# A chunked delta rule with a GELU feed-forward: chunks of 64 tokens with two batches on the partitions, and 32x32 diagonal blocks inverted row by row on VectorE

## The chip, the cores and the metric

The kernel runs on one core of a Trainium2 chip. A core has five engines that matter here: TensorE (PE in the profile; its weight loads are listed apart as PEld), VectorE (DVE), ScalarE (ACT), GpSimd (POOL) and SyncE (SP, which here only issues DMAs). Each engine runs its own instructions in order and waits for the others by semaphores. The metric is the device time of one execution in microseconds (us). All arithmetic is in float32.

## The reference

```python
def _attn_ref(q, k, v, beta):                      # q, k, v: (4, 8, 768, 48), beta: (4, 8, 768)
    B, H, S, D = q.shape
    k_n = k / (np.linalg.norm(k, axis=-1, keepdims=True) + 1e-06)
    state = np.zeros((B, H, D, D), dtype=np.float32)
    y = np.zeros_like(q)
    for t in range(S):
        kt, vt, bt = (k_n[:, :, t], v[:, :, t], beta[:, :, t, None])
        y[:, :, t] = np.einsum('bhd,bhde->bhe', q[:, :, t], state)
        v_old = np.einsum('bhde,bhd->bhe', state, kt)
        state = state + bt[:, :, :, None] * np.einsum('bhd,bhe->bhde', kt, vt - v_old)
    return y

def _moe_ref(x, w_in, w_out):                      # x: (3072, 384), w_in: (384, 2048), w_out: (2048, 384)
    h = x @ w_in
    g = 0.5 * h * (1.0 + erf(h * np.float32(1.0 / np.sqrt(2.0))))
    return g @ w_out

# y is laid out as x: (B, H, S, D) -> (B*S, H*D)
```

The first part is a recurrence over 768 tokens for each of 32 batch-and-head pairs, with a 48x48 state; the second is a feed-forward over 3072 rows. Both kernels take the recurrence in chunks of C tokens. With N[j, i] = beta_j k_j.k_i and P[j, i] = k_j.q_i for j < i (0 elsewhere), and the state St at the chunk's start, a chunk is

    (I + N^T) U = V - K St,   W = beta U,   Y = Q St + P^T W,   St' = St + K^T W.

So each chunk and head needs the inverse of a unit triangular C x C matrix, or rather that inverse transposed, Z, as the left operand of a matmul.

## The kernel before

A chunk is 128 tokens, on the 128 partitions. There are 6 chunks, 4 batches and 8 heads. A unit is one batch's chunk with its 8 heads; a group is two units (two batches), 12 groups in all.

For each unit, `prep` takes the norms of K (GpSimd and VectorE) and writes the normed K; `transposed` turns K and Q with eight TensorE transposes (L200) and ScalarE copies them out; `grams` forms K K^T and K Q^T (psG, L211), which VectorE (L216) scales by beta and masks to N, and ScalarE and GpSimd (L220, L222) copy and mask to P.

The inverse is then built on TensorE by doubling, from blocks of 1 to blocks of 64: at each of six sizes, `join` forms the part of M X that the size joins (psI, masked by VectorE at L244), `update_x` and `update_z` form X M X and its transpose (psI), and VectorE subtracts them (L268, L270, L273). The two 64x64 diagonal blocks of a head lie one above the other on the partitions and use two diagonal quarters of the TensorE array. `last_join` and `last_z` (L280, L289) join 64 to 128. All psI matmuls but the last are issued in the helper at L231.

The state of a chunk runs through `against_state` (psK, L314, and W, L317), `solve` (psU, L322, and U, L325), `read` (psY, L345 and L349), `next_state` (psS, L334, and the state's sum, L338) and `turn` (psX, L357, which turns the unit's result into columns of xT). The feed-forward of a group is `fc1` (psH, L372, 16 times 3 matmuls of 256 columns, then GELU on ScalarE) and `fc2` (psO, L381, 16 matmuls of 384 columns for each unit).

The order is made in two steps. `interleave` merges lists of steps by their place in each list: while group i runs through its state, group i + 1 is inverted and group i - 1 is in the feed-forward. From that program the framework makes each engine's own order. At the start the weights arrive as float64 words and are decoded to float32 by five VectorE and two GpSimd instructions each (`decode`, L167 to L175), 28 pieces, between the first two groups' inverses:

```python
    interleave(inverse_steps(0), [(decode, n) for n in range(n_in)])
    load(2)
    interleave(state_steps(0), inverse_steps(1), [(decode, n) for n in range(n_in, NW)])
    for i in range(1, NG):
        load(i + 2)
        interleave(state_steps(i), inverse_steps(i + 1), ffn_steps(i - 1))
    interleave(ffn_steps(NG - 1))
```

## Time and profile before

| what | us |
|---|---|
| median of three runs | 1407.06 |
| lowest and highest of the three | 1398.52, 1407.37 |
| span of the profiled execution (first to last instruction) | 1391.1 |
| first matmul of the first group's state (psU) starts at | 108.6 |
| VectorE busy in 108 to 200 us | 69.4 of 92 |
| VectorE busy in 400 to 500 us | 33.3 of 100 |
| DMA, mean share of the 16 engines in 400 to 500 us | 0.07 |

The profile is of one execution; its span leaves out what lies before the first and after the last instruction. A group's row names line, engine, operation, output and inputs, contraction rows by output rows, the moving operand's shape and the count, then busy time, mean duration in ns, and idle time before it with what ended it. A timeline row gives start, duration, and how many instructions it merges. A row of the windows view gives the stretch, then busy time and count of PE, PEld, DVE, ACT and POOL, then the granted TensorE clock (1.00 is full speed), the share of the DMA engines and GB/s.

### The profile page before, as it was taken

How to read it: one execution, taken by the hardware profiler on the slowest of the kernel's cores; microseconds unless marked ns; L12 is line 12 of the kernel's file. 1: busy time of each engine (PE TensorE's matmuls, PEld its weight loads, DVE VectorE, ACT ScalarE, POOL GpSimd, SP SyncE). 2: the span in 40 equal slices, each digit the busy share in tenths (PEclk: the TensorE clock that was granted, in tenths of full speed). 3: DMA queues.
4: the chain of work that ended last, by engine and by line, in shares of the span. 5: the costliest groups of instructions: out<-in, count | busy, mean ns of one | idle time of the engine just before them, and what ended most of it. 6: DMA issues, size and time to landing. Idle time of an engine off the chain costs nothing.

```text
span 1391.1 us, 37806 instructions
## 1 busy us (share of the span) xinstructions
PE 1338.4 (96%) x17806; PEld 1097.2 (79%) x17806; DVE 513.9 (37%) x964; ACT 178.8 (13%) x386; POOL 218.9 (16%) x217
## 2 busy tenths in 40 slices
PE   2979889999999999999999999999999999999999
PEld 1879778778878878878878877887887887887876
DVE  5785874423323332342342343342332233333100
ACT  1101011021011102102102102102101110210211
POOL 8554461101101001011010010110100100100000
PEclk9985989999998998999998999999899899999999
DMA  8322220010010001001001001001000000000000
GB/s 148 91 86 69 83 57 13 14 30 8 10 33 7 8 13 30 2 19 29 3 19 24 8 14 29 8 13 30 7 2 13 1 3 7 7 2 8 6 12 12
DMA packets 82571, 33.97 MB, mean 24 GB/s; under 512 B 75728, under 2 KB 78800, under 8 KB 82416
## 3 DMA queue, kind: packets, MB, share of 16 engines
q1 hardware_dynamic: 78912, 26.75, 8.7%
q10 hardware_dynamic: 3504, 4.82, 1.0%
q8 instruction: 139, 2.28, 0.7%
q14 instruction: 16, 0.13, 0.0%
HBM read 26.84 MB, written 4.72 MB: 23 GB/s over the span
## 4 chain that ended last, share of the span: by engine, by line
PE 90%; DVE 5%; POOL 3%; ACT 1%; issue 1%; ACTq 0%; POOLq 0%
PE psI L231 28%; PE psH L372 20%; PE psO L381 19%; PE psG L211 8%; PE psU L322 4%; PE psY L349 3%; PE psI L289 2%; PE psI L280 2%; POOL w_e L171 2%; PE psY L345 1%; PE psT L200 1%; PE psK L314 1%; PE psX L357 1%; DVE w_e L173 1%; PE psS L334 1%; DVE X L268 1%
## 5 line engine op out<-in xcount | busy, mean ns | idle before, releaser
L372 PE MATMUL psH<-xT,w_in_sb 128*128 128x256 f32 x1152 | 303.3, 402 | 0.0
L381 PE MATMUL psO<-w_out_sb,g 128*128 128x384 f32 x768 | 268.7, 496 | 0.0
L372 PEld LDWEIGHTS psH<-xT,w_in_sb 128*128 128x128 f32 x1152 | 209.6, 194 | 32.9
L381 PEld LDWEIGHTS psO<-w_out_sb,g 128*128 128x128 f32 x768 | 139.2, 190 | 84.3
L244 DVE TENSOR_TENSOR T<-psI,join 128x512 f32<-128x512 f32 x144 | 99.1, 688 | 182.0 <-PE psI L231 181.5
L231 PEld LDWEIGHTS psI<-T,Z 64*64 64x64 f32 x3456 | 121.5, 135 | 34.2 <-issue 21.5
L231 PEld LDWEIGHTS psI<-Z,T 64*64 64x64 f32 x3840 | 122.6, 136 | 26.7 <-issue 17.4
L231 PE MATMUL psI<-Z,T 64*64 64x64 f32 x3840 | 135.6, 220 | 7.7 <-DVE T L244 3.6
L231 PE MATMUL psI<-T,Z 64*64 64x64 f32 x3456 | 136.8, 221 | 5.6 <-DVE X L268 3.3
L231 PEld LDWEIGHTS psI<-X,N 64*64 64x64 f32 x3840 | 120.4, 136 | 22.0 <-issue 15.7
L231 PE MATMUL psI<-X,N 64*64 64x64 f32 x3840 | 131.1, 221 | 3.8 <-DVE X L268 3.5
L375 ACT ACTIVATE g<-psH 128x256 f32<-128x256 f32 x192 | 73.7, 384 | 473.3 <-PE psH L372 473.3
L268 DVE TENSOR_TENSOR X<-X,psI 128x512 f32<-128x512 f32 (+1 forms) x120 | 82.2, 685 | 134.4 <-PE psI L231 133.7
L211 PE MATMUL psG<-KQt 48*128 48x128 f32 x768 | 119.2, 329 | 1.2
L211 PEld LDWEIGHTS psG<-KQt 48*128 48x128 f32 x768 | 103.5, 226 | 13.9 <-ACT KQt L201 4.0
L191 POOL TENSOR_TENSOR Kp<-K,rn 128x384 f32<-128x384 f32 x24 | 19.9, 831 | 467.5 <-PE psS L334 466.4
L222 POOL TENSOR_SCALAR_AFFINE_SELECT P<-P 128x1024 f32<-128x1024 f32 x24 | 26.3, 1094 | 403.5 <-ACT P L220 403.5
L270 DVE TENSOR_TENSOR Z<-Z,psI 128x512 f32<-128x512 f32 x96 | 65.9, 687 | 58.0 <-PE psI L231 58.0
L216 DVE SCALAR_TENSOR_TENSOR N<-psG,beta_sb,mask_u 128x128 f32<-128x128 f32 x192 | 53.0, 343 | 72.3 <-PE psG L211 71.4
L171 POOL TENSOR_SCALAR w_e<-w_e 128x384 uint32<-128x384 uint32 (+1 forms) x28 | 53.8, 1921 | 71.2 <-DVE w_e L167 70.3
L273 DVE TENSOR_TENSOR ZF<-Z,psI 64x512 f32<-64x512 f32 x48 | 32.9, 685 | 61.9 <-PE psI L231 61.6
L231 PE MATMUL psI<-ident_c,N 64*64 64x64 f32 x768 | 45.9, 260 | 7.9 <-DVE N L216 7.9
(75 smaller groups left out, 1014.5 us busy)
## 6 DMA issues: line engine op xcount, KB each, us to landing
w_raw<-in_moe_w_in_dram SPq DMA_DIRECT2D x12, 512.0 KB, 3.7
w_raw<-in_moe_w_out_dram SPq DMA_DIRECT2D x16, 384.0 KB, 3.1
K<-in_k_dram SPq DMA_DIRECT2D x24, 192.0 KB, 3.1
Qp<-in_q_dram SPq DMA_DIRECT2D x24, 192.0 KB, 3.5
V<-in_v_dram SPq DMA_DIRECT2D x24, 192.0 KB, 3.0
out_dram<-o_sb ACTq DMA_DIRECT2D x24, 192.0 KB, 1.9
bt<-in_beta_dram ACTq DMA_DIRECT2D x1, 96.0 KB, 3.0
```

Of the source, the lines that this page charges most:

```text
L171: nc.gpsimd.tensor_scalar(e, e, 896.0, 1151.0, op0=ALU.max, op1=ALU.min)
L211: nc.tensor.matmul(psG[:, j, :], lhsT=u.KQt[pr, 0, j, :], rhs=u.KQt[pr, a, j, :], start=True, stop=True)
L216: nc.vector.scalar_tensor_tensor(u.N[:, hh, j, :], psG[:, j, :], beta_sb[:, u.c, u.b, h:h + 1], mask_u, ALU.mult, ALU.mult)
L231: nc.tensor.matmul(psI[HALF[g], n, :], lhsT=lhsT(g, n), rhs=rhs(g, n), start=True, stop=True)
L244: nc.vector.tensor_tensor(u.T, psI, joins[s].unsqueeze(1).to_broadcast([128, H, HB]), op=ALU.mult)
L268: nc.vector.tensor_tensor(u.X[pr], u.X[pr], dX[pr], op=ALU.subtract)
L270: nc.vector.tensor_tensor(u.Z, u.Z, psI, op=ALU.subtract)
L322: nc.tensor.matmul(psU[:, h, :], lhsT=ZF[u.slot][:, (h % 2) * NP + h // 2, :], rhs=u.W[:, h, :], start=True, stop=True)
L349: nc.tensor.matmul(psY[:, h, :], lhsT=u.P[:, h % 2, h // 2, :], rhs=u.U[:, h, :], start=(u.c == 0 and h == 0), stop=True, skip_group_check ...
L372: nc.tensor.matmul(psH, lhsT=w_in_sb[:, m, f * 128:(f + 1) * 128], rhs=xTs[i][:, m, :], start=(m == 0), stop=(m == NM - 1))
L375: nc.scalar.activation(gs[f], psH, ACT.Gelu)
L381: nc.tensor.matmul(u.psO, lhsT=gs[f][:, u.n * C:(u.n + 1) * C], rhs=w_out_sb[:, f, :], start=(f == 0), stop=(f == NF - 1))
```

## The change

A chunk has 64 tokens, so there are 12 chunks, and a unit holds the same chunk of two batches, one on partitions 0 to 63 and one on 64 to 127. A chunk has two units (four batches), and the work goes chunk by chunk. Two neighbouring chunks form a group of the inverse: 4 units x 8 heads = 32 places, each with two batches and two 32x32 diagonal blocks of N.

`flip` transposes on VectorE, for each of the four quarters of the partitions, 32 blocks of 32x32 in one instruction (L254), so that a partition then holds one block of one place as a 32x32 matrix along its free dimension. `eliminate` inverts all 128 blocks at once, row by row: for j from 1 to 30 one multiply (L261) and one add (L263) over (31 - j) j elements. `back` turns the result back, into Z (L275) and, for the upper blocks, into XM (L277). `join` then makes the off-diagonal 32x32 block of each 64x64 inverse with two levels of 32x32 matmuls on TensorE (psJ, L297 and L300), copied out by ScalarE (L306, L309). The six doubling steps, the joins to 128 and their masks go.

N and P are both masked by VectorE out of one pair of banks (L241, L243); the mask times minus beta is made by GpSimd (L214). A gram matmul is 64 rows of output and 128 columns (K and Q side by side). All state matmuls (psK L334, psU L345, psY L355 and L360, psS L372) work on 64 partitions, two or four tiles in turn. K is loaded straight into its padded tile and normed in place, with six such tiles (three chunks); `load` of chunk c + 2 is called at the start of chunk c, and its K tiles are those of chunk c - 1. Each load and each store is split in two, one for each batch. The staging of the first weights lies in the tile of the second weights; a decode writes in place.

`interleave` now takes a weight for each step, and merges by the sums of weights. The elimination of the next group stands in odd chunks, beside the state of the chunk, the grams of chunk c + 2 and the feed-forward of chunk c - 1. The feed-forward (psH L400, psO L409) does what it did, on 12 groups.

```diff
-    C = 128
-    HB = 64
-    SIZES = (1, 2, 4, 8, 16, 32)
+    C = 64
+    HB = 32
...
+    def fetch_in(dst, src, u):
+        rows = slice(u.c * C, (u.c + 1) * C)
+        for p in range(2):
+            nc.sync.dma_start(out=dst[HALF[p]],
+                              in_=src[2 * u.a + p, :, rows, :].rearrange("h t d -> t h d"))
+
+    def load(c):
+        if c >= NC:
+            return
+        for a in range(NA):
+            u = tiles[c, a] = Unit()
+            u.c, u.a, u.n = c, a, c * NA + a
+            u.t = (c % 2) * NA + a
+            u.Kp, u.Qp, u.bm = Kp[u.n % NKS], Qp[u.n % NQS], bm[u.n % 2]
+            fetch_in(u.Kp[:, :, 0:D], k, u)
+            fetch_in(u.Qp[:, :, 0:D], q, u)
...
+    def prep(c):
+        us = [tiles[c, a] for a in range(NA)]
+        rn = wk.tile([128, NA * H], F32, tag="rn", name="rn")
+        for u in us:
+            kd = u.Kp[:, :, 0:D]
+            ksq = wk.tile([128, H, D], F32, tag="ksq", name="ksq")
+            nc.gpsimd.tensor_tensor(ksq, kd, kd, op=ALU.mult)
+            nc.vector.tensor_reduce(rn[:, u.a * H:(u.a + 1) * H], ksq, axis=AX.X, op=ALU.add)
+        nc.gpsimd.tensor_tensor(rn, rn, half, op=ALU.pow)
+        nc.vector.tensor_scalar_add(rn, rn, 1e-6)
+        nc.vector.reciprocal(rn, rn)
+        for u in us:
+            kd = u.Kp[:, :, 0:D]
+            nc.gpsimd.tensor_tensor(
+                kd, kd, rn[:, u.a * H:(u.a + 1) * H].unsqueeze(2).to_broadcast([128, H, D]),
+                op=ALU.mult)
+        for u in us:
+            nc.gpsimd.tensor_tensor(
+                u.bm, mask_h, beta_m[:, u.c, u.a].unsqueeze(2).to_broadcast([128, H, C]),
+                op=ALU.mult)
+    def transposed(u):
+        u.KQt = wk.tile([128, NP, 2, 2, C], F32, tag="KQt", name="KQt", bufs=6)
+        psT = dn("psT").rearrange("q b (j n) -> q b j n", j=NP)
+        for x, src in ((0, u.Kp), (1, u.Qp)):
+            flat = src.rearrange("q h d -> q (h d)")
+            for j in range(NP):
+                nc.tensor.transpose(psT[:, x, j, :], flat[:, j * 128:(j + 1) * 128], ident)
+        for x in range(2):
+            nc.scalar.copy(u.KQt[:, :, :, x, :],
+                           psT[:, x].rearrange("q j (p n) -> q j p n", p=2))
...
+        psG = dn("psG").rearrange("q r (j n) -> q r j n", j=NP)
+        for j in range(NP):
+            for r, p in QUADS:
+                rows = slice(r * C, r * C + D)
+                nc.tensor.matmul(psG[HALF[p], r, j, :], lhsT=u.KQt[rows, j, p, 0, :],
+                                 rhs=u.KQt[rows, j, p].rearrange("q x n -> q (x n)"),
+                                 start=True, stop=True)
+        nc.vector.tensor_tensor(heads(Ns[g][:, u.t]), psG[:, :, :, 0:C], heads(u.bm),
+                                op=ALU.mult)
+        nc.vector.tensor_tensor(heads(u.P), psG[:, :, :, C:], heads(mask_h), op=ALU.mult)
+
+    def eliminate_steps(g):
+        steps = []
+
+        def flip(qd):
+            if qd == 0:
+                Nus[g] = wk.tile([128, HB, HB], F32, tag="Nu", name="Nu", bufs=1)
+            rows = slice(qd * HB, (qd + 1) * HB)
+            cols = slice((qd % 2) * HB, (qd % 2 + 1) * HB)
+            src = Ns[g][rows].rearrange("q t h n -> q (t h) n")[:, :, cols]
+            nc.vector.transpose(Nus[g][rows], src.rearrange("q u n -> q n u"))
+
+        def eliminate(j):
+            nu = Nus[g]
+            n = HB - 1 - j
+            tmp = wk.tile([128, HB * HB // 4], F32, tag="tmp", name="tmp")
+            tmp = tmp[:, 0:n * j].rearrange("q (i c) -> q i c", i=n)
+            nc.vector.tensor_tensor(tmp, nu[:, j + 1:, j:j + 1].to_broadcast([128, n, j]),
+                                    nu[:, j:j + 1, 0:j].to_broadcast([128, n, j]), op=ALU.mult)
+            nc.vector.tensor_tensor(nu[:, j + 1:, 0:j], nu[:, j + 1:, 0:j], tmp, op=ALU.add)
+
+        def diagonal():
+            flat = Nus[g].rearrange("q i c -> q (i c)")
+            nc.vector.memset(flat[:, 0:HB * HB:HB + 1], 1.0)
+
+        def back(qd):
+            nu = Nus[g]
+            if qd == 0:
+                XMs[g] = wk.tile([128, NU, HB], F32, tag="XM", name="XM", bufs=1)
+            rows = slice(qd * HB, (qd + 1) * HB)
+            cols = slice((qd % 2) * HB, (qd % 2 + 1) * HB)
+            nc.vector.transpose(Zf[g % 2][rows, :, cols].rearrange("q u i -> q i u"), nu[rows])
+            if qd % 2 == 0:
+                nc.vector.transpose(XMs[g][rows].rearrange("q u c -> q c u"),
+                                    nu[rows].rearrange("q i c -> q c i"))
+
+        steps = [(1.1, flip, qd) for qd in range(4)]
+        steps += [(0.5, eliminate, j) for j in range(1, HB - 1)]
+        steps += [(0.1, diagonal)]
+        steps += [(1.6, back, qd) for qd in range(4)]
+        return steps
+
+    def join(g, cc, level):
+        xm, zf, np_ = XMs[g], Zf[g % 2], Ns[g].rearrange("q t h n -> q (t h) n")
+        psJ = dn("psJ")
+        us = range(cc * NA * H, (cc + 1) * NA * H)
+        span = slice(us[0], us[-1] + 1)
+        for i, u in enumerate(us):
+            for p in range(2):
+                top = slice(p * C, p * C + HB)
+                low = slice(p * C + HB, (p + 1) * C)
+                col = slice(i * HB, (i + 1) * HB)
+                if level == 0:
+                    nc.tensor.matmul(psJ[low, 0, col], lhsT=np_[top, u, HB:C],
+                                     rhs=xm[top, u, :], start=True, stop=True)
+                else:
+                    nc.tensor.matmul(psJ[top, 0, col], lhsT=xm[low, u, :],
+                                     rhs=zf[low, u, HB:C], start=True, stop=True)
+        for p in range(2):
+            top = slice(p * C, p * C + HB)
+            low = slice(p * C + HB, (p + 1) * C)
+            if level == 0:
+                nc.scalar.copy(xm[low, span, :],
+                               psJ[low, 0].rearrange("q (u n) -> q u n", n=HB))
+            else:
+                nc.scalar.copy(zf[top, span, HB:C],
+                               psJ[top, 0].rearrange("q (u n) -> q u n", n=HB))
...
-    def join(u, s):
...
-    def update_x(u, s):
...
-    def update_z(u, s):
...
-    def last_join(u):
...
-    def last_z(u):
...
+            for p in range(2):
+                nc.tensor.matmul(psK[HALF[p], 2 * j:2 * j + 2, :], lhsT=u.KQt[:, j, p, 0, :],
+                                 rhs=St[:, u.a, p, j], start=True, stop=True)
+        u.W = wk.tile([128, H, D], F32, tag="W", name="W")
+        nc.vector.tensor_tensor(u.W, psK, u.V, op=ALU.subtract)
...
+        psU = sq("psU", H, D)
+        for h in range(H):
+            for p in range(2):
+                nc.tensor.matmul(psU[HALF[p], h, :], lhsT=zf[HALF[p], u.t * H + h, :],
+                                 rhs=rhs[HALF[p], h, :], start=True, stop=True)
+        u.U = wk.tile([128, H, D], F32, tag="U", name="U")
+        nc.vector.tensor_tensor(u.U, psU, b.unsqueeze(2).to_broadcast([128, H, D]), op=ALU.mult)
...
+        psS = dn("psS")
+        for j in range(NP):
+            for r, p in QUADS:
+                nc.tensor.matmul(psS[HALF[r], p, j * D:(j + 1) * D],
+                                 lhsT=u.Kp[HALF[p], 2 * j + r, :], rhs=u.U[HALF[p], 2 * j + r, :],
+                                 start=True, stop=True)
+        for r in range(2):
+            state = St[HALF[r], u.a, :, :, r, :]
+            nc.vector.tensor_tensor(
+                state, state,
+                psS[HALF[r], :, 0:NP * D].rearrange("q p (j d) -> q p j d", d=D), op=ALU.add)
...
+    def interleave(*lists):
+        merged = []
+        for m, steps in enumerate(lists):
+            total = sum(s[0] for s in steps)
+            at = 0.0
+            for s in steps:
+                merged.append(((at + 0.5 * s[0]) / total, m, s[1:]))
+                at += s[0]
+        for _, _, (fn, *args) in sorted(merged, key=lambda e: e[:2]):
+            if fn is not None:
+                fn(*args)
+
+    load_v(0)
+    for n in range(NS):
+        fetch(n)
+    interleave(gram_steps(0) + gram_steps(1) + inverse_steps(0),
+               [(1.0, decode, n) for n in range(6)])
+    load(2)
+    load_v(1)
+    interleave(state_steps(0), gram_steps(2), [(1.0, decode, n) for n in range(6, n_in)])
+    for c in range(1, NC):
+        load(c + 2)
+        if c + 1 < NC:
+            load_v(c + 1)
+        more = gram_steps(c + 2) + (inverse_steps(c // 2 + 1) if c % 2 else [])
+        if c == 1:
+            interleave(state_steps(c), more, ffn_steps(c - 1),
+                       [(1.0, decode, n) for n in range(n_in, NW)] + [(1.4 * NF, None)])
+            start.close()
+        else:
+            interleave(state_steps(c), more, ffn_steps(c - 1))
+    interleave(ffn_steps(NC - 1))
```

How the order changes is seen at two places. First TensorE, in the steady part. Before, where a unit's result is read (psY is the state, psI the inverse, psH and psO the feed-forward):

```order
L345 MATMUL psY<-S_bd,KQt 128x96 x4
L349 MATMUL psY<-U,P 128x48 x8
L231 MATMUL psI<-X,N 64x64 x16
L372 MATMUL psH<-xT,w_in_sb 128x256 x3
L231 MATMUL psI<-T,Z 64x64 x16
L231 MATMUL psI<-Z,T 64x64 x16
```

The state and a few psH stand between blocks of psI. In the changed kernel, late in an odd chunk (psJ is the join's 32x32 work, psS the state's sum):

```order
L409 MATMUL psO<-w_out_sb,g_2176 128x384
L297 MATMUL psJ<-XM,N 32x32 x32
L372 MATMUL psS<-U,Kp_71 64x48 x16
L409 MATMUL psO<-w_out_sb,g_2202 128x384
L409 MATMUL psO<-w_out_sb,g_2221 128x384
```

The join's matmuls stand among the last psO of the chunk, 32 at a time. And where a unit's result is read in the even chunk behind it:

```order
L345 MATMUL psU<-W,Zf_125 64x48 x16
L400 MATMUL psH<-xT,w_in_sb 128x256 x9
L355 MATMUL psY<-St,KQt 64x96 x8
L360 MATMUL psY<-U,P 64x48 x16
L224 MATMUL psT<-ident,Kp_71 128x128 x4
L224 MATMUL psT<-ident,Qp_77 128x128 x4
```

No psI stands between the feed-forward's blocks any more; the state's matmuls of 64 rows and the transposes for a later chunk's grams do.

Then VectorE, where the next inverse is made. Before, in one group (T, X and Z are the doubling's tiles, U the state's):

```order
L325 TENSOR_TENSOR U<-psU,beta_sb 128x384
L265 TENSOR_TENSOR Z<-ident_c,psI 128x512
L244 TENSOR_TENSOR T<-psI,join_134 128x512 x2
L268 TENSOR_TENSOR X<-X,psI 128x512
L270 TENSOR_TENSOR Z<-Z,psI 128x512
```

Each reads what TensorE has just written. After, in an odd chunk (P is the gram's second half, W the state's, Nu holds the 32x32 blocks one to a partition, tmp the product):

```order
L243 TENSOR_TENSOR P<-psG,mask 128x2x4x64
L254 STREAM_TRANSPOSE Nu<-N 32x1024
L337 TENSOR_TENSOR W<-psK,V 128x384
L254 STREAM_TRANSPOSE Nu<-N 32x1024 x3
L261 TENSOR_TENSOR tmp<-Nu 128x30
L263 TENSOR_TENSOR Nu<-Nu,tmp 128x30
L261 TENSOR_TENSOR tmp<-Nu 128x58
L263 TENSOR_TENSOR Nu<-Nu,tmp 128x29x2
```

The reads of psI have given way to operations from SBUF to SBUF that each take what the one before wrote. Further on in the same chunk:

```order
L263 TENSOR_TENSOR Nu<-Nu,tmp 128x2x29
L261 TENSOR_TENSOR tmp<-Nu 128x30
L263 TENSOR_TENSOR Nu<-Nu,tmp 128x30
L275 STREAM_TRANSPOSE Zf_125<-Nu 32x32x32
L277 STREAM_TRANSPOSE XM<-Nu 32x32x32
L275 STREAM_TRANSPOSE Zf_125<-Nu 32x32x32 x2
L277 STREAM_TRANSPOSE XM<-Nu 32x32x32
L275 STREAM_TRANSPOSE Zf_125<-Nu 32x32x32
L377 TENSOR_TENSOR St<-St,psS 64x8x48 x4
```

The transposes back stand behind the last add, and the state's sums (St) of that chunk behind the transposes.

More of the change, by code (lines that the diff above doesn't have):

```diff
@@ L330, in next_state @@
             return
-        psS = ps.tile([128, NP, D], F32, tag="seq", name="psS")
-        for h in range(H):
-            p0 = (h % 2) * HB
-            nc.tensor.matmul(psS[p0:p0 + D, h // 2, :], lhsT=Kp[u.slot][:, h, 0:D],
-                             rhs=u.U[:, h, :], start=True, stop=True)
-        for hh in range(2):
-            pr = slice(hh * HB, hh * HB + D)
-            nc.vector.tensor_tensor(S_bd[pr, u.b, :, hh, :], S_bd[pr, u.b, :, hh, :], psS[pr],
-                                    op=ALU.add)
```

359 lines of the change are left out of this document (127 added, 232 removed).

## The prediction

> **What bounds the kernel now.** I read the page's busy shares, slices and chain of waits first.
>
> ```profile
> PE 1338.4 (96%) x17806; PEld 1097.2 (79%) x17806; DVE 513.9 (37%) x964; ACT 178.8 (13%) x386; POOL 218.9 (16%) x217
> ...
> PE   2979889999999999999999999999999999999999
> ...
> DVE  5785874423323332342342343342332233333100
> ...
> PE 90%; DVE 5%; POOL 3%; ACT 1%; issue 1%; ACTq 0%; POOLq 0%
> ```
>
> TensorE is the bound: nines in every slice from the seventh on and 90% of the chain. VectorE is free two thirds of the time there. Only the first 200 us are mixed (weight decoding). So what counts is how much TensorE work goes, and whether VectorE can carry what replaces it. The groups by form say what TensorE does:
>
> ```profile
> L372 PE MATMUL psH<-xT,w_in_sb 128*128 128x256 f32 x1152 | 303.3, 402 | 0.0
> L381 PE MATMUL psO<-w_out_sb,g 128*128 128x384 f32 x768 | 268.7, 496 | 0.0
> L231 PE MATMUL psI<-T,Z 64*64 64x64 f32 x3456 | 136.8, 221 | 5.6 <-DVE X L268 3.3 <-DVE T L244 2.1
> L231 PE MATMUL psI<-Z,T 64*64 64x64 f32 x3840 | 135.6, 220 | 7.7 <-DVE T L244 3.6 <-DVE ZF L273 2.2 <-DVE Z L270 1.6
> L231 PE MATMUL psI<-X,N 64*64 64x64 f32 x3840 | 131.1, 221 | 3.8 <-DVE X L268 3.5 <-DVE Z L270 0.2
> L211 PE MATMUL psG<-KQt 48*128 48x128 f32 x768 | 119.2, 329 | 1.2
> ```
>
> The feed-forward (psH, psO) stays as it is; the inverse (psI) alone holds some 400 us here. Note the counts: 12 groups x 16 x 3 = 576 psH in the program, 1152 in the trace, so each float32 matmul is two records; I count records. A mean (402 ns) overlaps its neighbours, so paces come from the timeline, start to start:
>
> ```profile
> 523.89 0.60 PE L200 MATMUL psT<-ident,Kp 128*128 128x128 f32 x4
> 524.32 0.60 PE L200 MATMUL psT<-ident,Qp 128*128 128x128 f32 x4
> ...
> 554.42 2.08 PE L231 MATMUL psI<-X,N 64*64 64x64 f32 x64
> 556.43 1.56 PE L372 MATMUL psH<-xT,w_in_sb 128*128 128x256 f32 x6
> 557.93 1.15 PE L231 MATMUL psI<-T,Z 64*64 64x64 f32 x32
> 558.91 1.10 PE L231 MATMUL psI<-Z,T 64*64 64x64 f32 x32
> ...
> 593.65 0.56 PE L334 MATMUL psS<-U,Kp 128*48 128x48 f32 x16
> 594.15 2.08 PE L231 MATMUL psI<-X,N 64*64 64x64 f32 x64
> ...
> 1302.90 1.88 PE L322 MATMUL psU<-W,ZF 128*128 128x48 f32 x16
> 1304.61 2.82 PE L372 MATMUL psH<-xT,w_in_sb 128*128 128x256 f32 x12
> ...
> 1346.08 20.88 PE L372 MATMUL psH<-xT,w_in_sb 128*128 128x256 f32 x96
> 1366.80 20.80 PE L381 MATMUL psO<-w_out_sb,g 128*128 128x384 f32 x64
> ```
>
> - One feed-forward group, undisturbed: 20.7 + 20.8 = 41.5 us (217 and 325 ns a record, 0.85 ns a column).
> - A 64x64 record: 0.98/32 = 31 ns. Its 64 columns alone take 54 ns at 0.85, so the two diagonal tiles overlap.
> - psS, 48 weight columns, alternating column halves: 0.50/16 = 31 ns. psU, 128 weight columns: 1.71/16 = 107 ns for the same 48 columns streamed. psT: 0.43/4 = 108 ns.
> - Changing between full array and tiles: six psH take 1.50, not 1.30, and 64 psI 2.01, not 1.96: 0.25 us for there and back.
>
> **The change, TensorE's part.** All psI go. The state's matmuls become 64-row tiles in pairs, so I price 48 streamed columns at 31 ns (psS, psI) and 96 columns (psK, first half of psY) at 44 ns, the two-tile stream 96 x 0.85 / 2 plus a little. Per chunk: psU 64, psY 64, psS 64 records at 31 ns, psK 32 and psY 32 at 44 ns, psX 6 at 108 ns: 9.5 us. Grams: psT 16 at 108 ns and psG 64. A psG record streams 128 columns, 109 ns alone; on two tiles that is 54 ns, on four 27 ns. psS shows overlap of tiles that share rows, so I take 35 ns, near the four-tile end: 2.2 us, 3.9 us with psT (5.2 at the other end). Joins: psJ 256 records per group of two chunks, 32x32; no row shows that size, so bounds are 14 ns (32 columns at 0.85 on two tiles) and 62 (psI without its partner) and I take psI's 31 ns: 7.9 us.
>
> From chunk 2 on there are 11 feed-forwards (457), 10 states without the last psS (93), 8 grams (31) and 5 joins (40): 621 us. By the order about 109 trips between array and tiles come with it, at 0.25 us: 27 us (22 at 0.20).
>
> What TensorE no longer waits for (T, X, Z at a few us in the rows above) is small, since it was busy throughout. ScalarE loses the copies of P and of the last join and gains 8 short copies a group; it was busy 13% of the time, so nothing.
>
> **VectorE's part.** Per group: 4 transposes in, 30 pairs of multiply and add over (31-j)j elements, 4960 in each half, 6 transposes out.
>
> ```profile
> L244 DVE TENSOR_TENSOR T<-psI,join 128x512 f32<-128x512 f32 x144 | 99.1, 688 | 182.0 <-PE psI L231 181.5
> ...
> L325 DVE TENSOR_TENSOR U<-psU,beta_sb 128x384 f32<-128x384 f32 x24 | 13.4, 557 | 44.4 <-PE psU L322 44.4
> ...
> L174 DVE SCALAR_TENSOR_TENSOR w_f<-w_raw,w_m 128x512 f32<-128x512 uint32 x12 | 11.0, 913 | 0.0
> ...
> L132 DVE MEMSET S_bd<- 128x1536 f32 x1 | 1.3, 1338 | 0.3 <-issue 0.3
> ...
> 16.69 0.79 DVE L189 TENSOR_SCALAR rn<-rn 128x8 f32<-128x8 f32 x1 [1.44 <-POOL rn L188]
> 17.51 0.20 DVE L190 RECIPROCAL rn<-rn 128x8 f32<-128x8 f32 x1
> ```
>
> 512 against 384 elements: 131/128 = 1.02 ns each, and 0.16 us fixed. L190 depends on L189 and starts 0.03 after its end. So 60 dependent operations cost 60 x 0.195 + 9920 x 1.02 ns = 21.8 us. A transpose of 32 partitions x 1024 is in no row. At this rate it is 1.23 us; bounds are 0.9 (the memset's 0.87 ns an element) and 1.83 (L174's 913/512 = 1.78 ns, the slowest VectorE row of that width). I take 1.23, since the transpose reads one tensor and writes one, as plainly as L244 does: the inverse is 4.9 + 21.8 + 7.4 = 34 us.
>
> Is that hidden? In an odd chunk, psJ stands behind 48 psH and 20 psO of the program (33.9 us), 8 us of state, 3.9 of grams and 2.3 of trips: due at 48 us. VectorE's first transpose waits for the second psG's N, at about 11 us (12 psH 5.2, psT 1.7, psG 2.2, psK and trips 1.8), then does N and P 1.4, inverse 34, two W and two U 2.2: ready at 49 us. TensorE waits about 1 us, in four chunks after the start. If that cover is short, every further microsecond of the inverse is paid four times there. In the same stages K of chunk c+2 can only be loaded when psS of c-1 is done, and the norm's POOL step follows:
>
> ```profile
> L188 POOL TENSOR_TENSOR rn<-rn,half 128x8 f32<-128x8 f32 x24 | 39.6, 1649 | 15.1 <-DVE rn L187 15.1
> ```
>
> Twice as wide it is 3.3 us; with load and multiplies about 11 us against 10 us of cover: 1 us again. Eight us for these, five for hand-overs to ScalarE (gelu, xT, the join's copies are 0.5 us each and mostly covered): 13 us. The loads are twice as many DMAs of half the size, and SP's queue now holds a K load that waits for psS ahead of V and Q; both have a chunk's time, so I cost it at nothing beyond that 1 us.
>
> **Start.** VectorE decodes, and inverts groups 0 and 1, before chunk 2.
>
> ```profile
> L174 DVE SCALAR_TENSOR_TENSOR w_f<-w_raw,w_m 128x384 f32<-128x384 uint32 (+1 forms) x28 | 20.7, 738 | 0.0
> L173 DVE SCALAR_TENSOR_TENSOR w_e<-w_raw,w_e 128x384 uint32<-128x384 uint32 (+1 forms) x28 | 18.8, 673 | 16.8 <-POOL w_e L172 16.7
> ...
> L167 DVE TENSOR_SCALAR w_e<-w_raw 128x384 uint32<-128x384 uint32 (+1 forms) x28 | 12.4, 442 | 0.0
> L169 DVE TENSOR_SCALAR w_m<-w_raw 128x384 uint32<-128x384 uint32 (+1 forms) x28 | 12.2, 435 | 0.0
> ...
> L175 DVE SCALAR_TENSOR_TENSOR w_out_sb<-w_f,w_e 128x384 f32<-128x384 f32 x16 | 8.8, 549 | 0.0
> L175 DVE SCALAR_TENSOR_TENSOR w_in_sb<-w_f,w_e 128x512 f32<-128x512 f32 x12 | 8.3, 695 | 0.0
> ```
>
> Decoding 81, two inverses 68, 16 N and P 11, W, U and state 8, norms 5: 173 us, from about 22 us (5 us behind the first norm above) to 195. The program gives VectorE other work between dependent steps, which saves some gaps, and POOL's decode steps cost some; I let these cancel. psJ of group 1 at 192 us; 175 if the gaps saved win.
>
> **The clock.** It falls to half at times:
>
> ```profile
> 530.00:535.00 5.00, 4.88 (x49) 4.22 (x48) 2.41 (x10) 1.56 (x3) 1.09 (x1) 0.96 0.00 1
> 535.00:540.00 5.00, 5.00 (x36) 4.50 (x34) 0.65 (x3) 0.59 (x1) 0.00 (x0) 0.50 0.00 0
> ...
> 545.00:550.00 5.00, 5.00 (x77) 4.30 (x77) 1.93 (x3) 0.38 (x1) 1.27 (x1) 1.00 0.20 39
> ```
>
> TensorE was busy all of 535 to 540 us and its granted clock was still 0.50, in a run of psG and small psI with little psH between. Ten such us cost 5. The new order keeps psH or psO between all tile work, so I allow one: 5 us. The Trainium skill's "TensorE: Matmul & The Clock Gate", section "Why this matters for your kernels", asks only for no idle gaps over about 3 us; by that rule there would be no drop and 875. This trace has a drop without a gap, so the rule isn't enough here.
>
> **Sum.** 192 + 621 + 27 + 13 + 5 + 3.5 (last psO to the end, 1391.1 - 1387.6) = 862 us of span. Against the profiled 1391.1 the three runs were 7 to 16 us longer, the median 16; so about 880 us.
>
> **Rivals.**
> - VectorE's inverse becomes the bound. For it: dependent operations on a strided tile, none measured; two SBUF inputs beside a busy POOL (L174 takes 913 ns on 512 elements, L175 695). Against: 1.02 ns holds for every plain row. With the fixed cost doubled (+11.7) and transposes at 1.83 (+6) the inverse is 52 us, 18 more in four chunks and twice at the start: +108, 990 us (920 to 1060).
> - Tiles don't overlap: the 175 us of tile work doubles for its 150 us after the start: 1030 us. Against: psI's 31 ns for two row tiles that write one 2 KB tile (128x512 f32). The Trainium skill's "TensorEngine Tiling (Array Packing)", section "Gotcha 1: PSUM Pressure", says different row tiles cannot use one PSUM bank at once; the new psK, psU, psY and psJ do just that. By that rule, 1030; the trace disagrees, since psI did so at 31 ns.
> - The clock drops in most chunks: eight more times 5 us, 920.
> - Slower than before: the strided transposes are far dearer. All 60 are on the path at the margin; 529 us / 60 means it decides at 1.23 + 8.8 = 10 us each; at 11 us, 1466 us. Against: that is 10 ns an element, five times any VectorE row.
>
> **Numbers.** Forecast 0.68, VectorE's bound 0.20, no overlap 0.04, clock 0.06, slower 0.02. Low end: no waits, no drop, cheap trips and the early start take 40 off and the fastest run's overhead 9: 830. High end: 965 takes in the clock case and the nearer half of VectorE's case; above it lie 0.16 (0.10 of VectorE's case, no overlap, slower), below 830 some 0.03. Faster than 1% (about what can be told from no change) 0.98, within 0.005, slower 0.015.
>
> **What would show it.** Right: psU at 31 ns and psG near 35; multiply and add of some 0.2 + elements x 1.02 ns; transposes near 1.2 us; chunk 2 from about 190 us; pairs of chunks in some 125 us; TensorE busy to the end. Wrong: TensorE waiting many us for XM or N at psJ in odd chunks, tile records of 50 ns or more, half clock in most chunks.

## The result and the profile after

The kernel after takes 882.99 us (median of four runs, 881.35 to 884.01), the kernel before 1407.12 (four runs). The ratio is 0.630, 95% interval 0.627 to 0.633. The profiled execution has a span of 881.5 us and took 883.17.

The page of the kernel after: busy shares, then slices of TensorE, VectorE and the granted clock, and the head of the chain.

```profile
PE 733.3 (83%) x7444; PEld 543.9 (62%) x7444; DVE 402.4 (46%) x760; ACT 163.2 (19%) x362; POOL 153.7 (17%) x158
...
PE   3100087978999979999979999979999979999998
...
DVE  2888877987112991014980024970036950010000
...
PEclk9755568988999998999989999989999979999999
...
PE 57%; DVE 33%; POOL 5%; issue 2%; SPq 1%; DMA 1%; ACT 0%; POOLq 0%; DVEq 0%
```

TensorE's busy time fell from 1338 to 733 us, and its matmul records from 17806 to 7444. It is still the bound from the tenth slice on, but a dent comes back in every sixth slice or so, in busy time and clock alike, each just after VectorE's nines: the odd chunks with their inverse. VectorE's third of the chain is the start and these odd chunks, where the chain runs back through the inverse. The windows of an odd and an even chunk (busy time and count of PE, PEld, DVE, ACT, POOL; then clock, DMA share, GB/s):

```profile
276.00:340.00 64.00, 58.11 (x615) 43.18 (x616) 46.54 (x85) 12.02 (x28) 6.71 (x7) 0.95 0.13 26
340.00:404.00 64.00, 63.06 (x647) 45.98 (x646) 9.81 (x18) 14.74 (x33) 10.02 (x10) 1.00 0.13 26
```

The odd chunk loses 5.9 us idle and some 3 us to the clock, the even one 0.9 us. TensorE's timeline there:

```profile
320.18 0.68 PE L372 MATMUL psS<-U,Kp 64*64 64x48 f32 x32
320.79 2.85 PE L409 MATMUL psO<-w_out_sb,g 128*128 128x384 f32 x8
323.57 0.24 PE L297 MATMUL psJ<-XM,N 32*32 32x32 f32 x2
328.28 1.87 PE L297 MATMUL psJ<-XM,N 32*32 32x32 f32 x62 [4.47 <-DVE XM L277]
331.43 1.10 PE L372 MATMUL psS<-U,Kp 64*64 64x48 f32 x32 [1.28 <-DVE St L377]
332.47 4.19 PE L409 MATMUL psO<-w_out_sb,g 128*128 128x384 f32 x8
336.59 1.20 PE L297 MATMUL psJ<-XM,N 32*32 32x32 f32 x64
337.72 2.85 PE L409 MATMUL psO<-w_out_sb,g 128*128 128x384 f32 x8
```

VectorE's timeline of the same place:

```profile
318.82 1.95 DVE L275 STREAM_TRANSPOSE Zf<-Nu 32x1024 f32<-32x1024 f32 x1
320.64 1.99 DVE L277 STREAM_TRANSPOSE XM<-Nu 32x1024 f32<-32x1024 f32 x1
322.67 3.81 DVE L275 STREAM_TRANSPOSE Zf<-Nu 32x1024 f32<-32x1024 f32 x2
326.35 1.88 DVE L277 STREAM_TRANSPOSE XM<-Nu 32x1024 f32<-32x1024 f32 x1
328.26 1.90 DVE L275 STREAM_TRANSPOSE Zf<-Nu 32x1024 f32<-32x1024 f32 x1
330.17 1.12 DVE L377 TENSOR_TENSOR St<-St,psS 64x384 f32<-64x384 f32 x2
```

Read the two together. psJ waits 4.47 us until XM's second transpose has ended at 328.2. Then psS waits 1.28 us, because the state's sums (which free its PSUM buffer) stand in VectorE's queue behind the last transpose. After that, eight psO take 4.19 us instead of 2.85: half clock. From 276 us on this recurs in each of the four odd chunks that hold an inverse. The groups of transposes, and TensorE's waits of the stretch from 200 us (total, times, longest):

```profile
L254 DVE STREAM_TRANSPOSE Nu<-N 32x1024 f32<-32x1024 f32 x24 | 46.4, 1935 | 0.4
L275 DVE STREAM_TRANSPOSE Zf<-Nu 32x1024 f32<-32x1024 f32 x24 | 45.8, 1909 | 0.6
L277 DVE STREAM_TRANSPOSE XM<-Nu 32x1024 f32<-32x1024 f32 x12 | 23.2, 1932 | 0.0
```

```profile
PE psJ L297 <- DVE XM L277: 21.7, 5, 4.5
PE psS L372 <- DVE St L377: 5.0, 4, 1.3
PE psT L224 <- POOL Kp L210: 3.7, 4, 1.2
```

The third row is the wait for K and its norm, 0.7 to 1.2 us at the start of each of the four odd chunks (the one at 403 us lies in the window of the even chunk above); no drop of the clock follows it.

### The profile page after: what moved, and what is told of

The parts are those of the page before. It is cut to its first block, busy times and chain, and to the rows that moved or that the text cites. A ratio compares the mean times of both kernels' runs of the same rounds, so it can differ in the third digit from the quotient of the medians.

```text
span 881.5 us, 16758 instructions
## 1 busy us (share of the span) xinstructions
PE 733.3 (83%) x7444; PEld 543.9 (62%) x7444; DVE 402.4 (46%) x760; ACT 163.2 (19%) x362; POOL 153.7 (17%) x158
## 4 chain that ended last, share of the span: by engine, by line
PE 57%; DVE 33%; POOL 5%; issue 2%; SPq 1%; DMA 1%; ACT 0%; POOLq 0%; DVEq 0%
PE psO L409 21%; PE psH L400 20%; DVE Nu L263 7%; DVE tmp L261 6%; DVE Nu L254 5%; DVE Zf L275 4%; PE psT L224 3%; DVE XM L277 2%; PE psG L238 2%; POOL w_e L181 2%; PE psU L345 2%; PE psY L360 2%; PE psK L334 2%; DVE w_e L183 2%; PE psJ L300 2%
## 5 line engine op out<-in xcount | busy, mean ns | idle before, releaser
L409 PE MATMUL psO<-w_out_sb,g 128*128 128x384 f32 x768 | 273.4, 507 | 0.0
L400 PE MATMUL psH<-xT,w_in_sb 128*128 128x256 f32 x1152 | 268.5, 386 | 0.6 <-ACT xT L386 0.6
L400 PEld LDWEIGHTS psH<-xT,w_in_sb 128*128 128x128 f32 x1152 | 213.6, 191 | 32.3 <-issue 1.8
L409 PEld LDWEIGHTS psO<-w_out_sb,g 128*128 128x128 f32 x768 | 145.1, 196 | 92.4 <-issue 8.7
L297 PE MATMUL psJ<-XM,N 32*32 32x32 f32 x768 | 20.1, 214 | 105.9 <-DVE XM L277 105.8
L297 PEld LDWEIGHTS psJ<-XM,N 32*32 32x32 f32 x768 | 18.1, 128 | 112.5 <-issue 83.8
L263 DVE TENSOR_TENSOR Nu<-Nu,tmp 128x30 f32<-128x30 f32 (+9 forms) x180 | 62.8, 349 | 4.5
L261 DVE TENSOR_TENSOR tmp<-Nu 128x30 f32<-128x30 f32 (+9 forms) x180 | 61.4, 341 | 4.4
L214 POOL TENSOR_TENSOR bm<-mask,beta_m 128x512 f32<-128x512 f32 x24 | 25.4, 1063 | 209.5 <-DVE N L241 209.5
L241 DVE TENSOR_TENSOR N<-psG,bm 128x512 f32<-128x512 f32 x24 | 16.6, 691 | 90.4 <-PE psG L238 90.3
L254 DVE STREAM_TRANSPOSE Nu<-N 32x1024 f32<-32x1024 f32 x24 | 46.4, 1935 | 0.4
L275 DVE STREAM_TRANSPOSE Zf<-Nu 32x1024 f32<-32x1024 f32 x24 | 45.8, 1909 | 0.6
L377 DVE TENSOR_TENSOR St<-St,psS 64x384 f32<-64x384 f32 x44 | 24.3, 552 | 44.3 <-PE psS L372 43.8
L181 POOL TENSOR_SCALAR w_e<-w_e 128x384 uint32<-128x384 uint32 (+1 forms) x28 | 29.9, 1066 | 74.8 <-DVE w_e L177 74.7
L306 ACT COPY XM<-psJ 32x512 f32<-32x512 f32 x24 | 13.9, 578 | 156.3 <-PE psJ L297 154.6
L205 POOL TENSOR_TENSOR rn<-rn,half 128x16 f32<-128x16 f32 x12 | 35.2, 2933 | 14.1 <-DVE rn L204 14.1
L226 ACT COPY KQt<-psT 128x512 f32<-128x512 f32 x48 | 25.8, 590 | 41.4 <-PE psT L224 41.3
```

The source lines that it names most:

```text
L181: nc.gpsimd.tensor_scalar(e, e, 1151.0, 896.0, op0=ALU.min, op1=ALU.max)
L205: nc.gpsimd.tensor_tensor(rn, rn, half, op=ALU.pow)
L226: nc.scalar.copy(u.KQt[:, :, :, x, :], psT[:, x].rearrange("q j (p n) -> q j p n", p=2))
L254: nc.vector.transpose(Nus[g][rows], src.rearrange("q u n -> q n u"))
L261: nc.vector.tensor_tensor(tmp, nu[:, j + 1:, j:j + 1].to_broadcast([128, n, j]), nu[:, j:j + 1, 0:j].to_broadcast([128, n, j]), op=ALU.mult)
L263: nc.vector.tensor_tensor(nu[:, j + 1:, 0:j], nu[:, j + 1:, 0:j], tmp, op=ALU.add)
```

## The experiments

Theory: the tile work and the 60 dependent operations cost what was priced; the transposes cost 1.93 us, not 1.23, and that lengthens the start (two inverses) and the odd chunks, where each wait also brings a stretch of half clock. Rivals: the waits come from K's load and the norm; the lower clock comes from tile work as such; tiles do not overlap at all. Times of before in the three batches of runs were 1395.69, 1399.31 and 1395.51 us.

### Without the 60 multiplies and adds

```diff
-        steps += [(0.5, eliminate, j) for j in range(1, HB - 1)]
```

> Leaves out the 60 multiplies and adds of the row-by-row elimination (the inverse of a 32x32 block is then wrong); the ten transposes of a group stay. Theory: VectorE's inverse is what TensorE waits for at psJ in the odd chunks and what sets the start. The pairs take 21.6 us a group, so without them psJ is ready before it is due, the 4.5 us waits for XM and the half clock behind them go (4 x about 9 us), and the start is shorter by two times 21.6 us: 883 - 36 - 43 = 804, 795 to 825. Rival: the odd chunks' waits come from K's load and the norm on GpSimd, and the start from the decoding; then the waits stay where they are and less than half of this is gained: 850 or more.

Measured: 802.2 us in one run. From chunk 3 on TensorE waits for nothing but, near the end, 0.6 us for xT; the window of chunk 3:

```profile
227.00:288.00 61.00, 61.00 (x697) 45.10 (x696) 29.38 (x29) 14.51 (x32) 9.58 (x9) 1.00 0.14 27
```

The same tile work, without a gap, keeps a clock of 1.00. The last psX of chunks 2 and 8 start at 230.58 and 587.28 us, so a pair of chunks takes 118.9 us; in the kernel after they start at 274.95 and 658.70, 127.9 a pair. Of the 9.0 us between them, some 5.75 are the waits for VectorE (4.47 + 1.28), 0.9 the wait for K, which is gone here too, and the rest, about 2.4, is what the half clock leaves. The rival with K's load falls as the cause of the long waits: its own share is the 0.9.

### Every flip twice

```diff
-            nc.vector.transpose(Nus[g][rows], src.rearrange("q u n -> q n u"))
+            for _ in range(2):
+                nc.vector.transpose(Nus[g][rows], src.rearrange("q u n -> q n u"))
```

> Each of the four transposes of N into Nu is issued twice (the second writes the same values), 4 x 1.93 = 7.7 us more of VectorE a group. Theory: the transposes are on the path wherever psJ waits, so all of it is paid at the start (two groups) and in four odd chunks: 6 x 7.7 = 46 us, 929 (920 to 940); the longest wait of psJ for XM in an odd chunk grows from 4.5 to about 12 us. Rival: the wait at psJ is set by something else and VectorE has slack; then 883 to 898, from the start alone.

Measured: 902.0 us in one run, between the two. psJ of group 1 first starts at 222.9 us against 206.5: the 16 us expected of the start. But a pair takes 130.1 us, 2.2 more and not 7.7. TensorE's timeline in chunk 3 says why:

```profile
341.82 0.31 PE L298 MATMUL psJ<-XM,N 32*32 32x32 f32 x2 [7.54 <-DVE XM L278]
342.06 2.93 PE L410 MATMUL psO<-w_out_sb,g 128*128 128x384 f32 x4
344.99 1.11 PE L373 MATMUL psS<-U,Kp 64*64 64x48 f32 x32
```

The wait grew from 4.5 to 7.5 us, and in the new order psO and psS follow after two psJ records and cover the rest: the other 62 psJ were moved behind them. That the framework moved them because it counted the added work is likely, but not shown. "All of it is paid" was wrong for the odd chunks.

### The tiles' matmuls in a row

```diff
-        for h in range(H):
-            for p in range(2):
+        for p in range(2):
+            for h in range(H):
                 nc.tensor.matmul(psU[HALF[p], h, :], ...
```

and likewise in psG, psJ, psK, psY and psS.

> The same matmuls, but all of one 64x64 or 32x32 tile's matmuls stand in a row (the loop over the two batches, or over the four quarters, outermost) in psG, psJ, psK, psU, psY and psS, so that neighbours in the order use the same tile. Theory: the tiles overlap in the program as it is, psU 33 ns a record, psG 33, psS 19, psJ 18, psK 51; in a row a record costs at least its columns at 0.85 ns: psU and psS 41, psK 82, psG 109, psJ 27. Per chunk that is 2.4 (psU, psY, psS) + 2.0 (psK, psY) + 4.9 (psG) + 1.2 (psJ) = 10.5 us, over some ten chunks 105: about 990, 950 to 1030. Rival: row tiles that write one PSUM bank never overlap, so the order changes nothing: 883, within 1%.

Measured: 978.5 us in one run. From its timeline:

```profile
388.99 2.11 PE L300 MATMUL psJ<-Zf,XM 32*32 32x32 f32 x64
391.02 2.86 PE L400 MATMUL psH<-xT,w_in_sb 128*128 128x256 f32 x12
393.81 1.26 PE L334 MATMUL psK<-St,KQt 128*64 128x96 f32 x16
395.00 4.15 PE L400 MATMUL psH<-xT,w_in_sb 128*128 128x256 f32 x18
```

Start to start, psJ now takes 2.03/64 = 32 ns a record and psK 1.19/16 = 74; in turn they took 18 and 51. So neighbours on different tiles overlap: psK's, which differ in their columns of the array alone, and psJ's, which differ in rows and columns and write one PSUM bank on other partitions. The alternating order is worth some 95 us as a whole. A pair of chunks takes 141.0 to 142.7 us here, against 118.9 without waits, so the tiles alone give more, and the odd chunks' waits, about 1 us each here in place of 5.75, take some of it back.

### Joins later

```diff
-    return steps + [(2.0, join, g, cc, level) for level in range(2) for cc in range(2)]
+    return steps + [(0.8, join, g, cc, level) for level in range(2) for cc in range(2)]
```

> One number: the weight of a join in the merge goes from 2.0 to 0.8, so that psJ comes 8 to 9 psO of 0.7 us later in an odd chunk; nothing else is moved on purpose. Theory: the wait for XM (4.5 us) and most of the 1.3 us for the state's sum go, and with the gap the half clock that follows it for 8 to 9 us (about 4 us lost): 4 x 6 to 8 us, 883 - 28 = 855, 848 to 862; the granted clock of an odd chunk rises from 0.92 to 0.95 to about 1.00. Rival: the clock falls in that place from the tile work itself, gap or no gap; then the clock stays at 0.92 to 0.95 in odd chunks and only 4 x 4 us are won: 865 to 870. Second rival: the wait only moves to the next hand-over (Zf, XM's copies) in the same chunk: 875 to 883.

Measured: 868.6 us, ratio to before 0.621 (0.617 to 0.625), where the first rival had put it. The wait for XM is gone; one of 1.70 us is left, for the state's sums:

```profile
330.29 2.35 PE L297 MATMUL psJ<-XM,N 32*32 32x32 f32 x128 [1.70 <-DVE St L377]
```

and the clock still falls behind it, in the windows of the same run:

```profile
332.00:334.00 2.00, 2.00 (x49) 0.97 (x43) 0.34 (x1) 1.84 (x4) 1.58 (x1) 0.73 0.00 0
334.00:336.00 2.00, 2.00 (x65) 1.94 (x64) 0.43 (x2) 0.17 (x1) 1.33 (x2) 0.50 0.03 8
```

So the clock fell behind a gap of 1.7 us and 128 psJ in a row, for some 7 us in which TensorE was busy (10 in two of the other odd chunks). Whether the gap or the tile work did it, this run doesn't tell.

### XM first

```diff
-        steps += [(1.6, back, qd) for qd in range(4)]
+        steps += [(6.4 / 6, back, k) for k in range(6)]
```

with `back` taking XM's quarters 0 and 2 first, then Zf's 1, 3, 0, 2.

> Only the order of the six transposes at the end of an inverse changes: the two that write XM come first, then the four that write Zf. XM is then ready 5.8 us earlier (3 x 1.93), before TensorE asks for it. Theory: VectorE's queue as a whole is the limit there, because the state's sums stand behind all six transposes and the next psS needs the buffer that they free; so the wait for XM goes and one of about 6 us for the state's sum takes its place, with the same half clock behind it: 883, 876 to 888. Rival: XM is the only thing that is late; then 4 x 8 us are won: 850.

Measured: 886.1 us in one run: the wait moved, as the theory said. psJ starts unhindered, and psS stands instead:

```profile
321.42 1.20 PE L300 MATMUL psJ<-XM,N 32*32 32x32 f32 x64
329.87 1.11 PE L375 MATMUL psS<-U,Kp 64*64 64x48 f32 x32 [7.25 <-DVE St L380]
```

### Joins late, XM first, psS ahead of psY

```diff
-        steps = [(1.0, fn, u) for fn in (against_state, solve, read, next_state) for u in us]
+        steps = [(1.0, fn, u) for fn in (against_state, solve, next_state, read) for u in us]
```

with the two edits above. Its psY reads the state after the chunk, so it tests the order alone.

> Three moves and no other work: joins late as before (weight 0.8), XM's two transposes first, and in a chunk the state's sums (psS) ahead of the reading (psY), so that they no longer stand behind the transposes. Theory: all waits of the odd chunks from chunk 3 on go, and since the same tile work without a gap ran at a granted clock of 1.00 when the pairs were left out, the clock stays at 1.00 there: a pair of chunks takes the 118.9 us that it took without the pairs, against 127.9 now: 883 - 4 x 9 = 847, 840 to 856. Rival: the dense 32x32 tile work at the end of the chunk (two joins in a row) is what lowers the clock; then odd chunks keep a clock of 0.95 or less and the time is 858 to 866.

Measured: 844.8 us, ratio 0.602 (0.598 to 0.607). No wait of TensorE from 216 us on but 0.6 us for xT, a clock of 1.00 in every chunk from 264 us on, pairs of 118.5 us. Two of its windows, and its psJ:

```profile
264.00:327.00 63.00, 62.92 (x592) 45.55 (x591) 40.02 (x84) 11.50 (x27) 6.75 (x8) 1.00 0.14 28
327.00:385.00 58.00, 57.94 (x683) 42.93 (x683) 17.87 (x22) 15.21 (x33) 10.92 (x9) 1.00 0.15 29
...
331.78 2.21 PE L300 MATMUL psJ<-XM,N 32*32 32x32 f32 x128
```

Here too 128 psJ stand in a row, so in the odd chunks the tile work alone doesn't lower the clock, and the rival that had fitted "Joins later" falls: it takes the gap as well. What else decides it stays open (last section).

### What a transpose costs

```diff
+    bh = b.rearrange("q (u n) -> q n u", n=HB)
+    ah = a.rearrange("q (u n) -> q n u", n=HB)
...
+        for _ in range(6):
+            nc.vector.transpose(b[0:HB], a[0:HB])
+        for _ in range(6):
+            nc.vector.transpose(b, a)
...
+            nc.vector.transpose(b, ah)
...
+            nc.vector.transpose(bh, a)
```

> Adds a row of VectorE operations on two idle tiles behind the last inverse, six of each, to price the transpose: 32x1024 with both sides in plain order, 128x1024 plain, 32x512 plain, 128x1024 with the input in the strided order of the flips, 128x1024 with the output in the order of the turns back, and a plain copy of 128x1024. The total time is not the question. Theory: the 1.93 us is a rate of the transpose itself, about 1.8 ns an element of a partition and no strided penalty, and partitions are free: 1.9 us for all four forms of 1024 elements on 32 or 128 partitions, 1.0 us for 512. Rival one: the stride costs it, and the plain form takes 1.1 to 1.3 us, as I had priced it. Rival two: it goes by 32x32 blocks, so that 128 partitions take four times as long, 7.7 us. The copy takes 0.6 to 1.2 us.

The groups (idle tiles ma and mb; L462 and L464 plain, L466 half as long, L468 with strided input, L470 with strided output; the copy, L472, took 694 ns):

```profile
L468 DVE STREAM_TRANSPOSE mb<-ma 128x1024 f32<-128x1024 f32 x6 | 11.8, 1960 | 0.2
L470 DVE STREAM_TRANSPOSE mb<-ma 128x1024 f32<-128x1024 f32 x6 | 11.7, 1957 | 0.2
L464 DVE STREAM_TRANSPOSE mb<-ma 128x1024 f32<-128x1024 f32 x6 | 7.4, 1240 | 0.1
L462 DVE STREAM_TRANSPOSE mb<-ma 32x1024 f32<-32x1024 f32 x6 | 7.4, 1230 | 13.5 <-ACT xT L386 13.4
...
L466 DVE STREAM_TRANSPOSE mb<-ma 32x512 f32<-32x512 f32 x6 | 4.2, 699 | 0.2
```

Rival one holds, and the theory's "no strided penalty" falls. A plain transpose takes the 1.23 us that I had priced; the stride, on either side, adds 0.72; 128 partitions cost what 32 do. The Trainium skill's "SBUF — State Buffer" (a note in the section "Door 1: The DMA port swizzle (why `[64,N]` ≈ `[32,N]`)") says that consecutive accesses are at full bandwidth within a 16-byte line and pay for each new line; the strided forms step 128 bytes, and the 1960 against 1240 ns agree. That the line's 16 bytes are the limit is not shown: no run here has a smaller step.

### Chunks of 64, but the inverse by doubling on TensorE

```diff
-        steps = eliminate_steps(g)
-        return steps + [(2.0, join, g, cc, level) for level in range(2) for cc in range(2)]
...
+        for pair in (us[0:2], us[2:4]):
+            for s in SIZES:
+                steps += [(1.0, join, u, g, s) for u in pair]
+                for u in pair:
+                    steps += [(1.0, update_x, u, s), (1.0, update_z, u, g, s)]
```

> The chunks of 64, the two batches on the partitions and all tiles stay, but the 64x64 inverses are built on TensorE by doubling (six sizes, 64x64 tiles, masks and sums on VectorE) as in the kernel before; no transposes, no row-by-row steps, no psJ. It splits the gain. Theory: doubling costs 16 matmuls of two records for each of 16 blocks of a unit, 512 x 31 ns = 15.9 us a unit, 381 us for 24 units; the odd chunks' waits (36 us), psJ (27 us) and part of the start go: 883 + 381 - 63 = 1200, 1150 to 1300 with half clock in the dense parts. Then of the 524 us some 320 come from moving the inverse to VectorE and 200 from the chunks of 64 and the tiles. Rival: the chunk's size and the tiles give next to nothing, and the time comes back to 1350 or more.

Measured: 1162.1 us in one run. Its page:

```profile
PE 1097.3 (95%) x18196; PEld 882.2 (76%) x18196; DVE 444.6 (38%) x732; ACT 134.3 (12%) x314; POOL 180.6 (16%) x206
```

So of the gain, about 237 us (1399.3 - 1162.1) come with the chunks of 64, the two batches on the partitions and their tiles, and 279 us (1162.1 - 883.0) with moving the inverse to VectorE. I had expected 200 and 320. The 237 hold the smaller inverse too, since the joins from 64 to 128 go with the long chunks. TensorE's busy time divides in the same way: 241 us less, then 364 less, of which the waits and the half clock of the kernel after give some back.

### A version without the gaps, and with fewer transposes

The first of two, with joins at 0.8 and XM first as above:

```diff
-        return steps + [(0.5, turn, u) for u in us]
+        return steps + [(0.5, turn, u) for u in us] + [(2.0, None)]
```

> As the kernel after, all of its computation in place, with three numbers and an order changed: joins at weight 0.8, an empty step of weight 2 at the end of the state's steps (so that psS and its sums come some 8 us earlier in a chunk), and XM's two transposes first. The kernel without gaps (e6) had moved psS ahead of psY, so that its psY read the state after the chunk instead of before it; here the order of psY and psS is kept. Theory: the sums stand ahead of the last transposes, XM is ready before TensorE asks, nothing waits in the odd chunks, the clock stays at 1.00 from chunk 3 on: 845, 838 to 855. Rival: K's load and the norm, or the sums between the transposes, turn up as the next wait: 860 to 883.

Measured: 845.6 us, ratio 0.605 (0.602 to 0.608). The second one adds:

```diff
+        for qd in range(4):
...
+            nc.scalar.copy(Nds[g][rows, :, u.t * H:(u.t + 1) * H],
+                           Ns[g][rows, u.t, :, cols].rearrange("q h n -> q n h"))
...
+            nc.vector.transpose(Nus[g], Nds[g])
...
+                nc.vector.transpose(XMs[g].rearrange("q u c -> q c u"),
+                                    nu.rearrange("q i c -> q c i"))
...
+                nc.vector.transpose(zf[:, :, HB:].rearrange("q u i -> q i u"), nu)
+                nc.vector.transpose(zf[rows, :, 0:HB].rearrange("q u i -> q i u"), nu[rows])
```

> As the run beside it (sums early, joins late), and four transposes on 128 or 32 partitions in place of ten: ScalarE copies the diagonal blocks of N, in four copies a unit, into a tile in which a 128x1024 transpose reads them in plain order (1.24 us by the last run, against 4 x 1.93), XM is one transpose of 128 partitions (its lower quarters are overwritten by the join, 1.96), Zf one of 128 into the right half (its upper quarters are overwritten by the join) and two of 32 into the left half. 1.24 + 4 x 1.95 = 9.0 us a group against 19.2. Theory: the start is VectorE's and holds two groups, so 20 us go there, less about 2 for the copies; in the odd chunks it is hidden: 845 - 18 = 827, 818 to 838. Rival: the start is set by the decoding on GpSimd or by the weights' transfers; then the gain is under 8 us: 837 to 845.

Measured: 827.9 us, ratio 0.592 (0.590 to 0.595), the fastest here. Its transposes:

```profile
L276 DVE STREAM_TRANSPOSE XM<-Nu 128x1024 f32<-128x1024 f32 x6 | 12.3, 2057 | 0.2
L279 DVE STREAM_TRANSPOSE Zf<-Nu 128x1024 f32<-128x1024 f32 x6 | 11.5, 1913 | 0.0
L257 DVE STREAM_TRANSPOSE Nu<-Nd 128x1024 f32<-128x1024 f32 x6 | 7.5, 1245 | 9.7 <-ACT Nd L248 9.7
```

and 64 us of it, from within the inverse of an odd chunk (chunk 3, up to 312 us) into the next chunk:

```profile
276.00:340.00 64.00, 63.95 (x750) 47.72 (x740) 36.20 (x81) 17.91 (x39) 7.21 (x6) 1.00 0.12 23
```

psX of chunk 2 is 16.7 us earlier than in the first version (254.6 against 271.3), which is nearly all of the 17.8 us between them: the start was VectorE's.

## Why the prediction was right, and where it was not

880 us were predicted and 883.0 measured, but the nearness owes something to two errors of opposite sign: the span was put at 862 and was 881.5, and 16 us were added for what lies outside it, where the trace's own run had 1.7 (883.17 - 881.5). Behind the start, too, errors cancel: from the first psJ of group 1 to the end, 669.5 us were predicted (all terms but the 192) and 675.0 measured (881.5 - 206.5), with cheaper tile work and dearer waits than in the sum. So the mechanism was right, and the closeness to 3 us was luck.

- **Fewer matmuls, TensorE still the bound.** Right. The windows of even chunks are full, and the feed-forward took what it did before (the last 96 psH 20.8 us, start to start, against 20.7).
- **Tile paces.** Start to start in the kernel after, psU takes 1.07/32 = 33 ns a record (priced 31), psG 1.04/32 = 33 (35), psK 0.81/16 = 51 (44), psS 0.61/32 = 19 (31), psJ 1.13/64 = 18 (31). The rows of psS and psJ stand in TensorE's timeline above; those of psK and psU, each with the row after it, are:

```profile
287.93 0.88 PE L334 MATMUL psK<-St,KQt 128*64 128x96 f32 x16
288.74 5.45 PE L400 MATMUL psH<-xT,w_in_sb 128*128 128x256 f32 x24
294.12 1.14 PE L345 MATMUL psU<-W,Zf 64*64 64x48 f32 x32
295.19 5.45 PE L400 MATMUL psH<-xT,w_in_sb 128*128 128x256 f32 x24
```

  The two that were dear in the sum, psS and psJ, make 1.5 and 3.4 us a pair. With some 20 trips (109 over 11 chunks), 5 us, the sum had about 123 us a pair without waits (83 + 19 + 7.8 + 7.9 + 5); 118.9 were measured. The rival "tiles don't overlap" falls by the 95 us of the experiment. It named psK among the row tiles; psK and the first half of psY contract over all 128 partitions (128*64 in their rows) and differ in columns alone, so psU, psJ and the rest of psY are what speaks against it.
- **The 60 dependent operations.** Right: 296.16 to 318.82 us in chunk 3 without two U of the state is 21.6 us, priced 21.8.
- **The ten transposes.** This is the term that was mis-sized: "I take 1.23, since the transpose reads one tensor and writes one, as plainly as L244 does". The rate was right and the word "plainly" wrong, since each has a strided side: 1.93 us, above even my upper bound of 1.83. Ten make 7.0 us a group.
- **psJ due at 48 us, ready at 49.** The due time was right: psJ came up 48.6 us behind the last psX of chunk 2 (274.95 to 323.6). It was ready at 53.3 (328.28). So 5.75 us a chunk were paid, not 1. That every further microsecond is paid did not hold: with every flip twice, 7.7 us more of VectorE cost 2.2 a pair.
- **K's load and the norm, 1 us in four chunks.** Right: 3.7 us in four. They are gone in the runs whose odd chunks have no wait for VectorE.
- **One drop of the clock, 5 us.** Wrong in number: behind the start there is one in each odd chunk with an inverse, about 2.4 us each and so 10 in all, after the waits of 4.5 and 1.3 us. The rival "the clock drops in most chunks" saw more drops but named no cause; with the gaps gone they are gone.
- **The start, 192 us.** psJ of group 1 began at 206.5. Two inverses with dearer transposes account for the 14 us; that the gaps saved and POOL's steps cancel fits this, but no run separates the two.
- **16 us outside the span.** Wrong: runs of the kernel before also lie 2 us above their own spans (1396.38 against 1394.3). What I took for time outside the span was the difference between executions.
- **The rival "VectorE's inverse becomes the bound"** had the right mechanism at the wrong price: its 18 us a chunk assumed a doubled fixed cost of the dependent operations, which did not come; 9 us a pair did.

## What to carry to other kernels

Price a transpose on VectorE by how its operands step through memory and not by its element count alone, and put it on 128 partitions if 32 cost the same. When one engine nearly covers another, look at the whole queue behind the late instruction: moving XM alone won nothing, moving the sums and the joins with it won 37 us. A gap on TensorE can cost more than itself: in the odd chunks here half clock followed it, and one place in the order was worth 9 us a pair, of which the waits are 6.6.

## What the runs showed of the hardware that was not expected

- A 32x32-block transpose of 1024 float32 elements a partition takes 1.23 to 1.24 us plain and 1.96 us with one strided side, on 32 or 128 partitions alike (0.70 us for 512 plain).
- A gap of 1.7 us was followed by some 7 us at a clock of 0.50 while TensorE was busy. The Trainium skill's "TensorE: Matmul & The Clock Gate", section "Why this matters for your kernels", asks for no gaps over about 3 us; by that rule nothing should have fallen here, so the rule isn't enough. Without a gap the same records ran at 1.00. The gap's length alone doesn't settle it either. With the tiles' matmuls in a row, a gap of 0.94 to 0.98 us stands in each of the four odd chunks, and two of them (372.85 and 656.58 us) have a drop of some 4 us behind it, the other two none. With the inverse by doubling, a gap of 2.29 us has a drop behind it at 627.67 us and none at 442.11. In the start of the kernel after, a gap of 0.34 us (217.87) amid some 190 psJ has a drop from 219 to 222 us behind it. What decides it stays open, as does the drop without a gap in the kernel before (535 to 540 us).
- 32x32 records on tiles in turn start every 18 ns, and 64x64 records of 48 columns every 19 ns on four tiles, 33 ns on two.
